# Batch 0's second attention by halves of the columns, with a new order of the opening

## The chip, the cores and the metric

The kernel runs on one core of a Trainium2 chip. The metric is the time of one execution on the device in microseconds (us), the median of several runs.

## The reference

Two stages follow each other. The first is an attention with packed keys: for 8 batches, 8 heads, 576 positions and a head width of 64, a set of 32 packed queries `p` attends to `k` and `v`, and then `q` attends to the packed result, which serves as keys and as values. The second is an MLP over the 4608 tokens of width 512 that the attention gives.

```python
scale = 1.0 / np.sqrt(q.shape[-1])
p_packed = softmax(scale * p @ k.T) @ v             # 8 x 8 x 32 x 64
x = softmax(scale * q @ p_packed.T) @ p_packed      # 8 x 8 x 576 x 64
x = x.transpose(0, 2, 1, 3).reshape(4608, 512)
h = x @ w_in                                        # 512 x 2048
g = s * np.maximum(h, 0.0) ** 2 + b
out = g @ w_out                                     # 2048 x 512
```

## The kernel before

The core works batch by batch. Everything on TensorE is in bf16. The last product of the attention is folded into the MLP: the packed result times `w_in` is formed first (`pw`, 2 x 128 rows, one for each packed query of each head, by 2048 columns), and the MLP's first layer then multiplies `pw` with the softmax weights `aT` (2 x 128 rows by 576 positions). The two halves of the 256 rows are called `qd` 0 and 1 in the code.

The order of the work of batches 0 to 2, and of the attention of batch 3, is written out as a string of words, `ORDER` (line 15). A loop (line 678) calls one function for each word. Each engine executes its own instructions in the order of the words; waits between engines come from the data and from the buffers. The numbers behind a word are the batch and a part. The words that matter here:

| word | function | what it does |
|---|---|---|
| kf, kc | load_first_k, cast_first_k | heads 0 to 3 of batch 0's k, as f32 through SP's queue, and its conversion on DVE and ACT |
| kh, k, q, v, qh | load, load_pairs | loads through POOL's queue, converted to bf16 on the way; qh.0.0 and qh.0.1 are four loads of two heads each |
| p, pp2, mask | load_p, twice_p, mask | load of p, its doubling on DVE, the identity for the transposes on POOL |
| win, wout | load_w_in, load_w_out | a quarter of w_in (two loads), a quarter of w_out |
| kT, qT, pT | prep_k, prep_q, prep_p | TensorE transposes, half of the heads each (pT all), and copies out of PSUM on ACT and DVE |
| s | first_scores | scores of the packed queries (24 matmuls) and their exponential on ACT |
| a | packed | packed result and its sums; after the second, `ppc`, `rd` and `rs` on DVE |
| c | second_scores | scores of q against the packed result (16 matmuls) into two PSUM tiles, one for each qd; an exponential of 576 columns on ACT for each |
| w | weights | for one qd: sums over each head by a matmul with ones, `ld` (logarithm) and `rcd` (exponential of its negative) on ACT, and the product `aT` on DVE |
| e | packed_w1 | a quarter of `pw`: 8 matmuls; qd 0 is scaled out of PSUM by ACT, qd 1 by DVE |
| E | packed_w | half of `pw` |
| m | mlp_in | 128 of the 2048 hidden columns for 576 positions: 4 matmuls of 288 columns, a Relu (`rlu`) on ACT, its square into `gT` on DVE |
| t | Out.step | two of the 16 matmuls (512 columns each) that give 128 rows of the output; after the last, DVE adds the bias and SP's queue stores |
| b | bias_step | two of the 16 matmuls of the bias row |
| four, three | four, three | a change of the PSUM tiles: at "four" one of the two rings of buffers goes over to three output tiles and the bias |
| qo, qD, kD, vo | order_q, dma_q, dma_k, order_v | reordering on DVE and transposes by DMA on SP's queue, for batches from 3 on |
| z | idle | one matmul of zeros, 512 columns, whose result nobody reads (not in the order before) |

PSUM tiles for all but the outputs come from `big()` (line 108), which takes two rings of two buffers in turn; after "four" one ring of two buffers is left, and after "three" there is one of three. A tile's buffer is free when its last reader is done. The raw q, k and v lie in five buffers (line 120), which are given in the order of the words to the next load when the batch's transposes, or the packed result, have used them.

For batch 0 the order before has c.0 (both qd, all columns), then w.0.0 and w.0.1 by qd, with the e's in between. Every m.0 sums over both qd, so it reads what both w's have written.

```python
mm(hps[:, hf, 0:HS], pw[b][:, qd, m * P:(m + 1) * P],
   aT[b][:, qd, hf * HS:(hf + 1) * HS], start=(qd == 0), stop=(qd == NQ - 1))
```

After the last word a loop over batches 3 to 7 (line 682) goes on with a fixed interleaving, which the change leaves alone. It begins with the first m of batch 3 and then s.4.0.

Of the kernel before, what the change touches and what calls it, by code (L numbers as in the profile page):

```python
# [7 lines left out]
F32 = mybir.dt.float32  # L8
BF16 = mybir.dt.bfloat16
AF = mybir.ActivationFunctionType  # L10
ALU = mybir.AluOpType
# [1 line left out]


ORDER = """
kf kh.0.1 p.0.1 kc v.0 mask kT.0.0 qh.0.0 qh.0.1 pp2.0.1 kT.0.1 pT.0 win.0 s.0.0 s.0.1 a.0.0 win.2
qT.0.0 qT.0.1 p.1.2 a.0.1 c.0 w.0.0 e.0.0 win.1 win.3 wout.0 k.1 w.0.1 e.0.1 q.1 wout.1 e.0.2 m.0.3
pp2.1.2 m.0.0 e.0.3 wout.2 m.0.7 m.0.1 m.0.12 m.0.15 m.0.10 m.0.5 m.0.2 v.1 m.0.14 sb four b.0
kT.1.0 t.2 kT.1.1 t.1 m.0.4 qT.1.0 wout.3 b.1 qT.1.1 t.2 b.2 m.0.6 m.0.13 b.3 m.0.11 k.2 q.2 p.2.8
pT.1 t.0 t.1 t.0 b.4 s.1.0 t.1 s.1.1 t.2 m.0.8 b.5 a.1.0 m.0.9 a.1.1 b.6 t.0 c.1 b.7 t.0 t.1 q.3  # L20
kT.2.0 e.1.0 t.2 t.1 w.1.0 pp2.2.8 v.2 t.1 k.3 t.0 w.1.1 qT.2.1 t.0 t.1 t.0 t.0 e.1.1 t.2 kT.2.1 t.2
t.1 t.2 t.2 m.1.0 m.1.3 v.3 three t.3 t.3 pT.2 e.1.2 m.1.2 qT.2.0 t.3 t.3 m.1.1 m.1.5 m.1.7 t.3
e.1.3 m.1.9 qo.3 qD.3 kD.3 s.2.0 t.3 t.4 k.4 m.1.14 pT.3 t.4 m.1.4 s.2.1 t.3 m.1.13 m.1.15 m.1.6
m.1.8 t.4 m.1.11 m.1.10 m.1.12 a.2.0 t.4 t.4 t.3 a.2.1 t.4 t.4 c.2 t.5 t.4 t.5 q.4 E.2.0 t.6 t.5
w.2.0 t.6 w.2.1 s.3.0 t.5 pT.4 t.6 t.6 vo.3 s.3.1 t.5 t.5 m.2.2 m.2.3 t.6 E.2.1 m.2.1 t.6 t.5 v.4
a.3.0 t.5 m.2.5 a.3.1 t.6 m.2.0 t.7 m.2.15 qo.4 t.7 m.2.4 m.2.9 t.7 qD.4 m.2.7 t.7 c.3 t.7 t.6 m.2.6
kD.4 m.2.14 m.2.10 m.2.13 t.7 w.3.0 t.8 t.7 t.8 E.3.0 t.8 t.7 t.8 w.3.1 t.8 E.3.1 t.8 m.2.11 vo.4
t.8 t.8 m.2.12 m.2.8
"""

@with_exitstack
def kernel(
# [21 lines left out]
    B, H, S, D = q.shape  # L54
    NP = p.shape[2]
    DM = H * D
    DFF = moe_w_in.shape[1]
    P = 128
    scale = 1.0 / float(D) ** 0.5

    R = 96
    NC = S // R
    CP = NC // 2
    HP = H // 2
    NQ = H // 4
# [4 lines left out]
    HS = S // 2  # L70
# [6 lines left out]
    attp = ctx.enter_context(tc.tile_pool(name="attp", bufs=1))  # L77
    atp = ctx.enter_context(tc.tile_pool(name="atp", bufs=2))
    smp = ctx.enter_context(tc.tile_pool(name="smp", bufs=2))
    ppw = ctx.enter_context(tc.tile_pool(name="ppw", bufs=2))  # L80
    ysp = ctx.enter_context(tc.tile_pool(name="ysp", bufs=3))
# [10 lines left out]
    def mm(*a, **kw):  # L92
        return tc.keep_in_program_order(nc.tensor.matmul(*a, **kw))  # L93

    def tr(*a, **kw):
        return tc.keep_in_program_order(nc.tensor.transpose(*a, **kw))  # L96
# [9 lines left out]
    vec, act, pool, sp = (Pinned(e) for e in (nc.vector, nc.scalar, nc.gpsimd, nc.sync))  # L106

    def big(dt=F32):
        w = NB if dt == F32 else 2 * NB
        rings["n"] += 1  # L110
        ps = rings["h"][rings["n"] % len(rings["h"])]
        return ps.tile([P, 2, w], dt, tag="h", name="hps")


    kn, qn, vn = {}, {}, {}
# [7 lines left out]
    def raw(name, b):  # L123
        if (name, b - 1) in mine and b > 3:
            mine[name, b] = mine[name, b - 1]
        else:
            mine[name, b] = spare.pop(0)
        return bufs[mine[name, b]][:]

    def give(name, b):  # L130
        if b < 3:
            spare.append(mine[name, b])
# [3 lines left out]
    def done(name, b):  # L136

        halves[name, b] = halves.get((name, b), 0) + 1
        if halves[name, b] == 2:
            give(name, b)  # L140
# [9 lines left out]
    def load_pairs(store, src, b, tag, half):  # L150

        if half == 0:
            store[b] = raw(tag, b).rearrange("r (h x) -> r h x", h=H)
        for h2 in range(2):
            h0 = HP * h2 + 2 * half
            pool.dma_start(
                out=store[b][:, h0:h0 + 2, :],
                in_=src[b, h0:h0 + 2].rearrange("h (r c) d -> r h (c d)", c=NC),
            )

    w_in_sb = wpool.tile([P, NKC, DFF], BF16, name="w_in_sb")
    w_out_sb = wpool.tile([P, NFF, NB], BF16, name="w_out_sb")
    gT = wpool.tile([P, NFF, 3 * S], BF16, name="gT")
# [32 lines left out]
    identb = constp.tile([P, P], BF16, name="identb")  # L196
# [7 lines left out]
    kT = [constp.tile([P, KW], BF16, name=f"kT{i}") for i in range(2)]  # L204
    qT = [constp.tile([P, NC, HP, R], BF16, name=f"qT{i}") for i in range(2)]
    pbd = [constp.tile([P, NQ, 4, 2, NP], BF16, name=f"pbd{i}") for i in range(2)]
    ppc = [constp.tile([P, HP, NP], BF16, name=f"ppc{i}") for i in range(2)]
# [6 lines left out]
    onesbd = constp.tile([P, P], BF16, name="onesbd")  # L214
# [16 lines left out]
    aT, pw, vr, qr, e1, e2, rd, rs = {}, {}, {}, {}, {}, {}, {}, {}  # L231
# [53 lines left out]
    def prep_q(b, half):  # L285
# [18 lines left out]
                vec.tensor_copy(out=dst, in_=src)  # L304
        done("qn", b)

    def dma_q(b):
        sp.dma_start_transpose(
            out=qT[b % 2][:].rearrange("p c h r -> p (c h) r"),
            in_=qr[b][:].rearrange("r c h x d -> r (c h x d)"),  # L310
        )
# [101 lines left out]
    def weights(b, qd):  # L413
# [8 lines left out]
        act.activation(out=rcd[:], in_=ld[:].rearrange("p a s -> p (a s)"), func=AF.Exp, scale=-1.0)  # L422
        vec.tensor_tensor(out=aT[b][:, qd, :], in0=e2[b][:, qd, :], in1=rcd[:], op=ALU.mult)

    def packed_mm(i, ch, outs):

        for hp in range(HP):
            for h2 in range(2):
                mm(
                    outs[h2][NP * hp:NP * hp + NP, :],  # L430
                    ppc[i][D * h2:D * h2 + D, hp, :],
                    w_in_sb[D * h2:D * h2 + D, hp, ch * NB:(ch + 1) * NB],
                    start=True,
                    stop=True,
                    tile_position=(D * h2, NP * hp),
                )
# [15 lines left out]
    def packed_w1(b, ch, on_act=True):  # L452

        i = b % 2
        if ch == 0:
            pw[b] = ppw.tile([P, NQ, DFF], BF16, tag="pw", name="pw")
        t = big()
        packed_mm(i, ch, [t[:, qd, :] for qd in range(NQ)])
        dst = pw[b][:, :, ch * NB:(ch + 1) * NB]
        if on_act:  # L460
            act.activation(out=dst[:, 0], in_=t[:, 0, :], func=AF.Copy, scale=rd[b][:, 0:1])
        else:
            vec.tensor_scalar_mul(out=dst[:, 0], in0=t[:, 0, :], scalar1=rd[b][:, 0:1])
        vec.tensor_scalar_mul(out=dst[:, 1], in0=t[:, 1, :], scalar1=rd[b][:, 1:2])
# [4 lines left out]
    def slot(b):  # L469
        return 1 if b % 2 else (b % 4)  # L470
# [5 lines left out]
    def mlp_in(b, m, on_act=True):  # L476
        hps = big()
        for qd in range(NQ):
            for hf in range(2):
                mm(  # L480
                    hps[:, hf, 0:HS],
                    pw[b][:, qd, m * P:(m + 1) * P],
                    aT[b][:, qd, hf * HS:(hf + 1) * HS],
                    start=(qd == 0),
                    stop=(qd == NQ - 1),
                )
        g0 = slot(b) * S
        dst = gT[:, m, g0:g0 + S].rearrange("p (a s) -> p a s", a=2)
        if on_act:
            rlu = ysp.tile([P, 2, HS], BF16, tag="rlu", name="rlu")  # L490
            act.activation(out=rlu[:], in_=hps[:, :, 0:HS], func=AF.Relu)
            vec.tensor_tensor(out=dst, in0=rlu[:], in1=rlu[:], op=ALU.mult)
        else:
            vec.scalar_tensor_tensor(
                out=dst, in0=hps[:, :, 0:HS], scalar=0.0, in1=hps[:, :, 0:HS],
                op0=ALU.max, op1=ALU.mult,
            )

    def bias_part(bps, m0, m1):
        for m in range(m0, m1):  # L500
            mm(bps, onesb[:], w_out_sb[:, m, :], start=(m == 0), stop=(m == NFF - 1))
        if m1 == NFF:
            vec.tensor_scalar_mul(out=biasrep[:], in0=bps, scalar1=bvec[:])
# [109 lines left out]
    y = outs(0) + outs(1) + outs(2)  # L613
# [22 lines left out]
    def constants():  # L636
        sp.dma_start(out=svec[:], in_=moe_s[0:1].unsqueeze(0).to_broadcast([P, 1]))
        sp.dma_start(out=bvec[:], in_=moe_b[0:1].unsqueeze(0).to_broadcast([P, 1]))

    words = {  # L640
        "k": lambda b: load(kn, k, b, "kn"),
        "q": lambda b: load(qn, q, b, "qn"),
# [14 lines left out]
        "pp2": lambda b0, b1: twice_p(b0, min(b1, B)),  # L657
        "pT": prep_p,
        "kT": prep_k,
        "qT": prep_q,  # L660
        "kD": dma_k,
        "qo": order_q,
        "qD": dma_q,
        "vo": order_v,
        "s": first_scores,
        "a": packed,
        "c": second_scores,
        "w": weights,
        "e": packed_w1,
        "E": packed_w,  # L670
        "m": lambda b, m: mlp_in(b, m),
        "n": lambda b, m: mlp_in(b, m, False),
        "t": lambda t: y[t].step(2),
        "b": bias_step,
# [7 lines left out]
    for b in range(3, B):  # L682
        a = b + 1
        c = a + 1
# [23 lines left out]
        for m in range(NFF):  # L708
            mlp_in(b, m)
            for f in steps.get(m, []):  # L710
                f()
            run_outs(todo, per)
# [33 lines left out]
```

## Time and profile before

| | |
|---|---|
| time, median of 7 runs | 259.12 us (258.93 to 259.52) |
| the profiled execution: its own time | 258.93 us |
| its span in the profile | 257.1 us |
| TensorE (PE) busy | 240.7 us, 94% |
| ScalarE (ACT) busy | 145.3 us, 57% |
| VectorE (DVE) busy | 144.1 us, 56% |
| GpSimd (POOL) busy, mostly issuing loads | 31.4 us, 12% |
| moved by DMA | 34.61 MB, 135 GB/s in the mean |

The span reaches from the first instruction to the last; the execution's own time has 1.8 us more around it. PE is TensorE's matmuls and PEld its loads of weights, which overlap with them. [...]what a group costs is read from the distance between starts. SP's queue and POOL's queue are those that issue transfers. Times in a timeline count from the start of the span.

### The profile page before, as it was taken

The page shows a single profiled execution, that of the slowest core. Times are in us where ns is not written, and L with a number is a line of the kernel's source. Part 1 is how long each engine was busy: PE and PEld are TensorE (multiplying, and loading weights), DVE is VectorE, ACT ScalarE, POOL GpSimd, SP SyncE. Part 2 cuts the span into 40 slices and gives each one's busy share as a digit, 9 for nine tenths or more (in the row PEclk, how much of TensorE's full clock was granted, in tenths as well). Part 3 has the DMA queues.
Part 4 walks back from the last instruction along what each step waited for, and adds up shares of the span by engine and source line. Part 5 has one row for each costly group of instructions (what it writes and reads, how often), then busy time and mean ns, then how long its engine had stood idle before and what let it go on. Part 6 is the DMA issues. An engine that isn't in the chain of part 4 may idle for free.

```text
span 257.1 us, 5606 instructions
## 1 busy us (share of the span) xinstructions
PE 240.7 (94%) x2320; PEld 138.2 (54%) x2320; DVE 144.1 (56%) x299; ACT 145.3 (57%) x220; POOL 31.4 (12%) x47
## 2 busy tenths in 40 slices
PE   1476999999999999999999999999999999999994
PEld 1461556556655664665566455655565555555443
DVE  3324853576765877857854668366835473444212
ACT  3038946456848688848763674569554764444000
POOL 8366230110002100300030003000000000000000
PEclk9999999999999999999999999999999999999999
DMA  5999999999398969993979397946611113111332
GB/s 108 180 204 203 204 206 205 198 199 247 75 160 132 174 133 163 158 234 79 187 101 220 96 177 120 236 91 134 135 43 41 43 41 87 41 41 41 84 82 82
DMA packets 54858, 34.61 MB, mean 135 GB/s; under 512 B 27568, under 2 KB 50352, under 8 KB 54832
## 3 DMA queue, kind: packets, MB, share of 16 engines
q0 software_dynamic: 24864, 18.32, 48.2%
q1 hardware_dynamic: 29872, 15.87, 27.4%
q8 instruction: 18, 0.29, 0.4%
q10 hardware_dynamic: 96, 0.07, 0.1%
q14 instruction: 8, 0.07, 0.1%
HBM read 37.23 MB, written 9.44 MB: 181 GB/s over the span
## 4 chain that ended last, share of the span: by engine, by line
PE 84%; DMA 13%; POOL 1%; issue 1%; DVE 0%; POOLq 0%
PE yps L93 50%; PE hps L93 33%; DMA w_out_sb<-in_moe_w_out_dram 6%; DMA w_in_sb<-in_moe_w_in_dram 4%; DMA raw<-in_k_dram 3%; PE hps L96 1%; POOL raw L104 1%; POOL w_in_sb L104 0%; DVE ysb L104 0%; POOLq L730 0%
## 5 line engine op out<-in xcount | busy, mean ns | idle before, releaser
L93 PE MATMUL yps<-w_out_sb,gT 128*128 128x512 bf16 (+2 forms) x592 | 144.6, 374 | 0.0
L104 ACT ACTIVATE rlu<-hps 128x576 bf16<-128x576 f32 x128 | 80.8, 651 | 63.2 <-PE hps L93 57.2
L104 DVE TENSOR_TENSOR gT<-rlu 128x576 bf16<-128x576 bf16 x128 | 58.2, 457 | 62.0 <-ACT rlu L104 60.0
L93 PE MATMUL hps<-aT,pw 128*128 128x288 bf16 x512 | 81.1, 289 | 0.1
L93 PEld LDWEIGHTS <-gT 128*128 128x128 bf16 x592 | 53.2, 98 | 48.6 <-issue 6.4
L93 PEld LDWEIGHTS <-pw 128*128 128x128 bf16 x512 | 49.8, 99 | 33.9 <-issue 1.3
L104 DVE SCALAR_TENSOR_TENSOR ysb<-yps,svec,biasrep 128x512 f32<-128x512 f32 (+2 forms) x37 | 27.0, 732 | 16.6 <-PE yps L93 16.5
L104 DVE TENSOR_SCALAR pw<-hps,rd 128x1024 bf16<-128x1024 f32 (+1 forms) x20 | 21.3, 1067 | 2.4 <-ACT pw L104 2.0
L104 ACT ACTIVATE pw<-hps,rd 128x1024 bf16<-128x1024 f32 (+1 forms) x20 | 18.7, 942 | 4.5 <-PE hps L93 3.7
L104 DVE TENSOR_TENSOR aT<-e,rcd 128x576 bf16<-128x576 bf16 x16 | 12.1, 758 | 13.1 <-ACT rcd L104 13.1
L104 POOL DMA_DIRECT2D raw<-in_k_dram x8 | 6.4, 802 | 94.4 <-DMA kT<-raw 83.5
L96 PE MATMUL hps<-identb,raw 96*64 96x96 bf16 (+1 forms) x216 | 9.9, 232 | 8.1 <-DVE raw L104 5.8
L104 ACT ACTIVATE e<-hps 96x768 bf16<-96x768 f32 x16 | 12.6, 800 | 8.1 <-PE hps L93 8.1
L104 ACT ACTIVATE e<-hps,rs 128x576 bf16<-128x576 f32 x16 | 11.0, 738 | 6.4 <-PE hps L93 6.4
L96 PEld LDWEIGHTS <-raw 96*64 96x64 bf16 (+1 forms) x216 | 8.5, 123 | 10.7 <-DVE raw L104 5.8
L93 PE MATMUL hps<-w_in_sb,ppc 64*32 64x512 bf16 x256 | 12.1, 410 | 1.4 <-DMA w_in_sb<-in_moe_w_in_dram 1.4
L104 ACT ACTIVATE rcd<-ld 128x576 f32<-128x576 f32 x16 | 10.9, 682 | 0.5
L104 ACT ACTIVATE ld<-hps 128x576 f32<-128x576 f32 x16 | 10.3, 646 | 1.2 <-PE hps L93 1.0
L104 DVE COPY raw<-raw 96x1536 bf16<-96x1536 bf16 x20 | 10.4, 562 | 0.0
L93 PEld LDWEIGHTS <-raw 96*64 96x64 bf16 (+1 forms) x264 | 8.4, 113 | 2.9 <-issue 2.1
L93 PE MATMUL hps<-e,raw 96*64 96x32 bf16 (+1 forms) x264 | 9.2, 194 | 0.8 <-ACT e L104 0.8
L93 PE MATMUL hps<-pbd,kT 128*128 128x64 bf16 x192 | 8.6, 199 | 1.1 <-DVE pbd L104 1.1
(41 smaller groups left out, 97.8 us busy)
## 6 DMA issues: line engine op xcount, KB each, us to landing
raw<-in_v_dram POOLq DMA_DIRECT2D x8, 576.0 KB, 12.2
out_dram<-ysb SPq DMA_DIRECT2D x23, 192.0 KB, 2.3
raw<-in_k_dram POOLq DMA_DIRECT2D x7, 576.0 KB, 6.7
raw<-in_q_dram POOLq DMA_DIRECT2D x7, 576.0 KB, 10.4
out_dram<-ysb SPq DMA_DIRECT2D x24, 128.0 KB, 2.4
w_in_sb<-in_moe_w_in_dram POOLq DMA_DIRECT2D x8, 256.0 KB, 9.4
w_out_sb<-in_moe_w_out_dram POOLq DMA_DIRECT2D x4, 512.0 KB, 16.5
out_dram<-ysb SPq DMA_DIRECT2D x23, 64.0 KB, 2.2
```

The source lines that it names most:

```text
L93: return tc.keep_in_program_order(nc.tensor.matmul(*a, **kw))
L96: return tc.keep_in_program_order(nc.tensor.transpose(*a, **kw))
L104: return lambda *a, **kw: tc.keep_in_program_order(f(*a, **kw))
```

## The change

Three things change.

For batch 0 the second scores and the softmax weights are made by halves of the columns instead of by qd. `second_scores_half` makes one half's scores for both qd in one PSUM tile (8 matmuls) and two exponentials of 288 columns. `weights_half` makes the sums, the logarithm, the reciprocal and the product of one half's columns for both qd. The word c.0 becomes c.0.0 and c.0.1, and w.0.0 and w.0.1 now stand for the halves. The words h.0.0 to h.0.15 replace m.0.0 to m.0.15: `mlp_in_half` takes 256 hidden columns for one half of the positions (h.0.x with even x for the first half), 4 matmuls of 288 columns, one Relu and one square each, as an m has.

For batch 0, qT goes by halves of the columns, all heads at once (`prep_q_chunks`); the loads of q stay four loads of two heads.

The order of the words is another up to the end of the string. In the opening the loads of q stand ahead of v, the quarters of w_in come in the order 0, 1, 2, 3, p.1.2 stands behind k.1, kT.0.1 is ahead of kT.0.0, and six idle matmuls (z) are added. f.0.0 and f.1.2 do the work of e.0.0 and e.1.2 with both qd scaled on DVE. Later, the loads of batches 2 and 3 come as q.2, k.2, p.2.8, q.3, v.3, k.3, v.2.

```diff
--- before.py
+++ after.py
@@ -13,19 +13,19 @@
 
 
 ORDER = """
-kf kh.0.1 p.0.1 kc v.0 mask kT.0.0 qh.0.0 qh.0.1 pp2.0.1 kT.0.1 pT.0 win.0 s.0.0 s.0.1 a.0.0 win.2
-qT.0.0 qT.0.1 p.1.2 a.0.1 c.0 w.0.0 e.0.0 win.1 win.3 wout.0 k.1 w.0.1 e.0.1 q.1 wout.1 e.0.2 m.0.3
-pp2.1.2 m.0.0 e.0.3 wout.2 m.0.7 m.0.1 m.0.12 m.0.15 m.0.10 m.0.5 m.0.2 v.1 m.0.14 sb four b.0
-kT.1.0 t.2 kT.1.1 t.1 m.0.4 qT.1.0 wout.3 b.1 qT.1.1 t.2 b.2 m.0.6 m.0.13 b.3 m.0.11 k.2 q.2 p.2.8
-pT.1 t.0 t.1 t.0 b.4 s.1.0 t.1 s.1.1 t.2 m.0.8 b.5 a.1.0 m.0.9 a.1.1 b.6 t.0 c.1 b.7 t.0 t.1 q.3
-kT.2.0 e.1.0 t.2 t.1 w.1.0 pp2.2.8 v.2 t.1 k.3 t.0 w.1.1 qT.2.1 t.0 t.1 t.0 t.0 e.1.1 t.2 kT.2.1 t.2
-t.1 t.2 t.2 m.1.0 m.1.3 v.3 three t.3 t.3 pT.2 e.1.2 m.1.2 qT.2.0 t.3 t.3 m.1.1 m.1.5 m.1.7 t.3
-e.1.3 m.1.9 qo.3 qD.3 kD.3 s.2.0 t.3 t.4 k.4 m.1.14 pT.3 t.4 m.1.4 s.2.1 t.3 m.1.13 m.1.15 m.1.6
-m.1.8 t.4 m.1.11 m.1.10 m.1.12 a.2.0 t.4 t.4 t.3 a.2.1 t.4 t.4 c.2 t.5 t.4 t.5 q.4 E.2.0 t.6 t.5
-w.2.0 t.6 w.2.1 s.3.0 t.5 pT.4 t.6 t.6 vo.3 s.3.1 t.5 t.5 m.2.2 m.2.3 t.6 E.2.1 m.2.1 t.6 t.5 v.4
-a.3.0 t.5 m.2.5 a.3.1 t.6 m.2.0 t.7 m.2.15 qo.4 t.7 m.2.4 m.2.9 t.7 qD.4 m.2.7 t.7 c.3 t.7 t.6 m.2.6
-kD.4 m.2.14 m.2.10 m.2.13 t.7 w.3.0 t.8 t.7 t.8 E.3.0 t.8 t.7 t.8 w.3.1 t.8 E.3.1 t.8 m.2.11 vo.4
-t.8 t.8 m.2.12 m.2.8
+z kf kc kh.0.1 mask p.0.1 qh.0.0 qh.0.1 kT.0.1 kT.0.0 z z v.0 z win.0 win.1 pp2.0.1 pT.0 qT.0.1 z
+s.0.0 s.0.1 qT.0.0 win.2 a.0.0 a.0.1 c.0.0 f.0.0 sb win.3 c.0.1 w.0.0 w.0.1 e.0.1 z h.0.2 h.0.0
+e.0.2 wout.0 q.1 h.0.4 h.0.7 h.0.5 e.0.3 h.0.6 h.0.8 wout.1 h.0.1 h.0.11 h.0.13 k.1 h.0.3 four
+h.0.10 t.1 p.1.2 h.0.9 wout.2 t.2 h.0.15 qT.1.1 t.1 t.2 qT.1.0 b.0 t.0 h.0.12 t.0 v.1 b.1 pp2.1.2
+t.1 kT.1.1 t.2 pT.1 wout.3 b.2 h.0.14 q.2 kT.1.0 t.1 t.0 t.0 b.3 s.1.0 s.1.1 t.0 t.1 k.2 t.1 p.2.8
+a.1.0 b.4 a.1.1 q.3 b.5 b.6 b.7 c.1 t.1 t.0 t.1 e.1.0 w.1.0 t.0 t.0 w.1.1 v.3 t.2 qT.2.1 t.2 e.1.1
+k.3 t.2 t.2 t.2 kT.2.0 pp2.2.8 m.1.0 three t.3 t.3 pT.2 kT.2.1 f.1.2 t.3 e.1.3 v.2 t.3 qT.2.0 t.3
+m.1.8 m.1.1 m.1.6 m.1.14 m.1.13 m.1.3 t.3 m.1.5 m.1.10 qo.3 m.1.2 t.4 qD.3 s.2.0 m.1.7 m.1.9 m.1.11
+t.4 s.2.1 m.1.4 m.1.12 kD.3 t.3 m.1.15 a.2.0 t.4 a.2.1 t.4 t.4 t.4 pT.3 k.4 c.2 t.4 t.4 t.3 E.2.0
+w.2.0 t.6 t.6 t.5 w.2.1 t.6 t.5 t.5 vo.3 t.6 E.2.1 t.6 m.2.5 t.5 t.5 t.6 pT.4 t.6 s.3.0 s.3.1 t.6
+m.2.1 t.5 m.2.3 a.3.0 m.2.13 t.5 m.2.10 a.3.1 t.7 q.4 t.7 t.7 c.3 t.5 qo.4 m.2.2 t.7 t.7 w.3.0 t.8
+t.8 E.3.0 qD.4 t.8 t.8 kD.4 w.3.1 v.4 t.7 m.2.14 t.7 m.2.0 m.2.15 m.2.6 m.2.7 m.2.9 t.8 t.8 m.2.12
+m.2.8 m.2.11 t.7 m.2.4 E.3.1 t.8 t.8 vo.4
 """
 
 @with_exitstack
@@ -157,6 +157,16 @@
                 out=store[b][:, h0:h0 + 2, :],
                 in_=src[b, h0:h0 + 2].rearrange("h (r c) d -> r h (c d)", c=NC),
             )
+
...
     w_in_sb = wpool.tile([P, NKC, DFF], BF16, name="w_in_sb")
     w_out_sb = wpool.tile([P, NFF, NB], BF16, name="w_out_sb")
@@ -298,6 +308,28 @@
         for x in range(2):
             dst = qT[i][:, :, 2 * half + x, :]
             src = tp[:, x, 0:S].rearrange("p (c r) -> p c r", c=NC)
+            if x == 0:
+                act.copy(out=dst, in_=src)
+            else:
+                vec.tensor_copy(out=dst, in_=src)
+        done("qn", b)
+
+    def prep_q_chunks(b, hf):
+
+        i = b % 2
+        tp = big(BF16)
+        for hp in range(HP):
+            for c in range(CP):
+                o = ((hp % 2) * CP + c) * R
+                for h2 in range(2):
+                    tr(
+                        tp[D * h2:D * h2 + D, hp // 2, o:o + R],
+                        qn[b][:, hp + HP * h2, (CP * hf + c) * D:(CP * hf + c + 1) * D],
+                        identb[0:R, 0:R],
+                    )
+        for x in range(2):
+            dst = qT[i][:, CP * hf:CP * hf + CP, 2 * x:2 * x + 2, :].rearrange("p c a r -> p a c r")
+            src = tp[:, x, 0:S].rearrange("p (a c r) -> p a c r", a=2, c=CP)
             if x == 0:
                 act.copy(out=dst, in_=src)
             else:
@@ -422,6 +454,46 @@
         act.activation(out=rcd[:], in_=ld[:].rearrange("p a s -> p (a s)"), func=AF.Exp, scale=-1.0)
         vec.tensor_tensor(out=aT[b][:, qd, :], in0=e2[b][:, qd, :], in1=rcd[:], op=ALU.mult)
 
+    def second_scores_half(b, hf):
+
+        i = b % 2
+        if hf == 0:
+            e2[b] = attp.tile([P, NQ, S], BF16, tag="e2", name="e2")
+        t = big()
+        for hp in range(HP):
+            for h2 in range(2):
+                mm(
+                    t[NP * hp:NP * hp + NP, h2, 0:HS],
+                    ppc[i][D * h2:D * h2 + D, hp, :],
+                    qT[i][D * h2:D * h2 + D, CP * hf:CP * hf + CP, hp, :],
+                    start=True,
+                    stop=True,
+                    tile_position=(D * h2, NP * hp),
+                )
+        for qd in range(NQ):
+            act.activation(
+                out=e2[b][:, qd, hf * HS:(hf + 1) * HS],
+                in_=t[:, qd, 0:HS],
+                func=AF.Exp,
+                scale=rs[b][:, qd:qd + 1],
+            )
+
+    def weights_half(b, hf):
+        if hf == 0:
+            aT[b] = atp.tile([P, NQ, S], BF16, tag="aT", name="aT")
+        cols = slice(hf * HS, (hf + 1) * HS)
+        dps = big()
+        for qd in range(NQ):
+            mm(dps[:, qd, 0:HS], onesbd[:], e2[b][:, qd, cols], start=True, stop=True)
+        ld = smp.tile([P, 2, HS], F32, tag="ld", name="ld")
+        act.activation(out=ld[:], in_=dps[:, :, 0:HS], func=AF.Ln)
+        rcd = smp.tile([P, S], F32, tag="rcd", name="rcd")
+        act.activation(out=rcd[:], in_=ld[:].rearrange("p a s -> p (a s)"), func=AF.Exp, scale=-1.0)
+        vec.tensor_tensor(
+            out=aT[b][:, :, cols], in0=e2[b][:, :, cols],
+            in1=rcd[:].rearrange("p (a s) -> p a s", a=2), op=ALU.mult,
+        )
+
     def packed_mm(i, ch, outs):
 
         for hp in range(HP):
@@ -495,6 +567,25 @@
                 out=dst, in0=hps[:, :, 0:HS], scalar=0.0, in1=hps[:, :, 0:HS],
                 op0=ALU.max, op1=ALU.mult,
             )
+
+    def mlp_in_half(b, x):
+
+        mp, hf = divmod(x, 2)
+        hps = big()
+        for y in range(2):
+            m = 2 * mp + y
+            for qd in range(NQ):
+                mm(
+                    hps[:, y, 0:HS],
+                    pw[b][:, qd, m * P:(m + 1) * P],
+                    aT[b][:, qd, hf * HS:(hf + 1) * HS],
+                    start=(qd == 0),
+                    stop=(qd == NQ - 1),
+                )
+        g0 = slot(b) * S + hf * HS
+        rlu = ysp.tile([P, 2, HS], BF16, tag="rlu", name="rlu")
+        act.activation(out=rlu[:], in_=hps[:, :, 0:HS], func=AF.Relu)
+        vec.tensor_tensor(out=gT[:, 2 * mp:2 * mp + 2, g0:g0 + HS], in0=rlu[:], in1=rlu[:], op=ALU.mult)
 
     def bias_part(bps, m0, m1):
         for m in range(m0, m1):
@@ -637,6 +728,7 @@
         sp.dma_start(out=svec[:], in_=moe_s[0:1].unsqueeze(0).to_broadcast([P, 1]))
         sp.dma_start(out=bvec[:], in_=moe_b[0:1].unsqueeze(0).to_broadcast([P, 1]))
 
+    by_halves = (0,)
     words = {
         "k": lambda b: load(kn, k, b, "kn"),
         "q": lambda b: load(qn, q, b, "qn"),
@@ -644,6 +736,7 @@
         "kh": lambda b, x: load(kn, k, b, "kn", 4 * x, 4 * x + 4),
         "qh": lambda b, x: load_pairs(qn, q, b, "qn", x),
         "vh": lambda b, x: load_pairs(vn, v, b, "vn", x),
         "kf": load_first_k,
         "kc": cast_first_k,
         "p": lambda b0, b1: load_p(b0, min(b1, B)),
@@ -657,18 +750,20 @@
         "pp2": lambda b0, b1: twice_p(b0, min(b1, B)),
         "pT": prep_p,
         "kT": prep_k,
-        "qT": prep_q,
+        "qT": lambda b, x: (prep_q, prep_q_chunks)[b in by_halves](b, x),
         "kD": dma_k,
         "qo": order_q,
         "qD": dma_q,
         "vo": order_v,
         "s": first_scores,
         "a": packed,
-        "c": second_scores,
-        "w": weights,
+        "c": lambda b, *x: (second_scores, second_scores_half)[b in by_halves](b, *x),
+        "w": lambda b, x: (weights, weights_half)[b in by_halves](b, x),
         "e": packed_w1,
+        "f": lambda b, ch: packed_w1(b, ch, False),
         "E": packed_w,
         "m": lambda b, m: mlp_in(b, m),
+        "h": mlp_in_half,
         "n": lambda b, m: mlp_in(b, m, False),
         "t": lambda t: y[t].step(2),
         "b": bias_step,
```

## The prediction

> **What bounds the kernel now.** I read the busy table and the slices first, then the chain of waits, then the timeline of the first 50 us, engine by engine. The page says that TensorE (PE) is the bound, and where it is not:
>
> ```profile
> PE 240.7 (94%) x2320; PEld 138.2 (54%) x2320; DVE 144.1 (56%) x299; ACT 145.3 (57%) x220; POOL 31.4 (12%) x47
> PE   1476999999999999999999999999999999999994
> ```
>
> Each slice is 6.4 us: after the fourth, PE is full to the end. The chain (start, us, what) says the same: transfers until 37.6 us, then PE.
>
> ```profile
> 1.30 7.76 DMA raw<-in_k_dram
> ...
> 9.95 10.03 DMA w_in_sb<-in_moe_w_in_dram
> ...
> 21.98 15.59 DMA w_out_sb<-in_moe_w_out_dram
> 37.61 0.59 PE yps L93 x2
> ```
>
> So the time is the PE work plus what PE loses in the opening. The timeline (start, us, engine, ...) shows the loss:
>
> ```profile
> 18.49 0.68 PE L93 MATMUL hps<-qT,ppc 64*32 64x288 bf16 x16 [0.56 <-DVE ppc L104]
> 19.23 1.37 ACT L104 ACTIVATE e<-hps,rs 128x576 bf16<-128x576 f32 x2 [1.49 <-PE hps L93]
> 22.10 0.76 DVE L104 TENSOR_TENSOR aT<-e,rcd 128x576 bf16<-128x576 bf16 x1 [3.38 <-ACT rcd L104]
> 23.93 0.76 DVE L104 TENSOR_TENSOR aT<-e,rcd 128x576 bf16<-128x576 bf16 x1 [0.41 <-ACT rcd L104]
> 24.76 2.10 PE L93 MATMUL hps<-aT,pw 128*128 128x288 bf16 x8
> 27.35 4.54 PE L93 MATMUL hps<-aT,pw 128*128 128x288 bf16 x32
> 28.23 4.61 ACT L104 ACTIVATE rlu<-hps 128x576 bf16<-128x576 f32 x8
> ```
>
> c.0 starts at 18.49, and no m.0 can start until both weight tiles (aT) are there, at 24.69. From 24.76 PE is busy, but the first matmuls of 288 columns come 240 ns apart (8 take 2.0 us) and only from 27.7 on 122 ns: half clock. Further small losses are waits for q.1 (0.3 us at 34.7) and w_out (0.4 at 37.2). By c.1, at 47.28, PE has done about 25.8 us of work in warm slots, so 21.5 us are lost by then; hardly anything after. A warm slot, from the timeline's start-to-start distances, is m 0.49 us, t and b 0.43, kT 0.51, qT 0.6, s 0.35, a 0.65, e 0.35, w 0.25.
>
> [...]240 against 122 ns, the switch 2.9 us after the m's begin. [...]from 13.98 to 17.93 us PE was never idle, half of it transposes, and stayed at half clock. [...]the POOL loads do land in their order of issue.[...]
>
> **The loads.** POOL has eight loads out at once (win.0's second half is issued at 9.34, after the first load landed at 9.06), and from 10 to 45 us the ring is never empty: the stage table has 201 to 205 GB/s there. So a load's landing is the sum of what is ahead of it. The trace's landings: kh 9.06, p 9.26, v 12.09, the four q parts 12.83 to 15.03, win 17.65, 20.93, 23.73, 26.35, wout.0 28.87, k.1 32.27, q.1 34.96, wout.1 37.56, wout.2 40.09, v.1 42.96, wout.3 45.49. Reordered: q parts by 12.2, v 15.0, win.0 17.65, win.1 20.9, win.2 23.5, win.3 26.1 (p.1.2, 0.24, goes back), wout.0 28.6, q.1 31.9, wout.1 34.5, k.1 37.3, wout.2 40.1, v.1 43.0, wout.3 45.5. The mask moved ahead of p delays issues by 0.3 us, nothing else, as kh is still in flight.
>
> **The change part by part, in cold slots until the clock switches.**
> 1. Before c.0.0. kT.0.1 now comes first and waits for kh: PE starts at 9.1, two kT (0.96 each) to 11.03, three idle matmuls (0.43 each) to 12.3, pT to 12.5, qT.0.1 to 13.5, idle to 13.9, two s (0.64 each) to 15.2, qT.0.0 to 16.2. The exponentials (2 x 0.8) end at 16.3, a.0.0 and a.0.1 (0.95 each) at 18.25, ppc and rs as before 0.7 to 0.9 later: c.0.0 at 18.9. **0.4 later than now**; of the six added idle matmuls (2.6 us) only the one before s, 0.43, is on the path, the others stand in gaps.
> 2. The halves. c.0.0 has 8 matmuls for 16; its two exponentials of 288 elements[...] run 19.4 to 20.3, those of c.0.1 20.2 to 21.05[...]. w.0.0 at 20.3, logarithm 21.05, reciprocal 21.7 to 22.4, product (0.76) to **23.2**: half of the columns for both qd. w.0.1 is done at 24.5. f.0.0 puts 0.7 us from ACT onto idle DVE. So h.0.2 starts at 23.25 against 24.76: **1.5 us earlier**.
> 3. h.0.2 and h.0.0 take 1.92 cold. e.0.2 then waits for a buffer: that of e.0.1, which DVE empties only after the second product, at 25.2. e.0.2 to 25.8, h.0.4 to 26.8. I let the clock switch at 27.0 (3.7 us after the h's start). Then h.0.7, h.0.5, e.0.3, h.0.6, h.0.8, h.0.1 run to 29.75. An h needs one 576-element Relu as an m does (0.575 apart on ACT against 0.49 on PE), so ACT paces; h.0.11 waits 0.45 for e.0.3's copies, and after "four", with two buffers left, t.1 starts at 32.2, qT.1.1 at 34.05, b.0 at 36.1.
> 4. From there slots add up, no load being late (kT.1.1 at 38.7 against k.1 37.3, a.1.0 at 45.0 against 43.0, b.6 at 47.2 against 45.5): c.1 at **48.05**. By then 14 t's and 8 b's are done, now 9 and 7: 6 x 0.43 = 2.6 us more work. The same work is done now at 47.28 + 2.6 = 49.9. **Gain 1.85 us.** Matmul work stays as it was (16 h are 128 matmuls, as 16 m).
> 5. Behind c.1 the order is new, and PE stays full if nothing is late. v.2 moves behind v.3 and k.3 and takes kT.2.1's buffer: issued at 57.6, landing some 10 us later as v.3 does now (56.5 to 66.4), needed by a.2.0 at 70.9. On SP, qD.4 and kD.4 stand behind t.5's stores: about 92.5, landed 101 (3.1 + 5.1), needed by s.4.0 at 103.6 (82.6 us of slots ahead of it and 21 lost); now 102.5 for 105.3. I cost these at nothing, on margins of 3 and 2.5 us; f.1.2 too, with DVE at 7.6 of 10 us there. The tail is untouched.
>
> The switch is the term that no row settles. At 30.7 nothing is left of the gain (each us of half clock costs 0.5). In the other direction, if the idle matmuls bring it by 18 us, a, c, w and the first h's run warm: some 1.3 us more. I take 27.0.
>
> Sum: the profiled execution, 258.93 (span 257.1 and 1.8 around it), becomes 257.1; the median of the runs is 0.2 above it: 257.3.
>
> **The rivals.**
> - Main case, 57%: 257.3 (256.5 to 258.4).
> - Early clock, 16%: the idle matmuls and s keep PE busy from 9.1 to 16.2. For it: no gap there, where now there are three. Against: over half of it are transposes (kT and qT, 3.9 of 7.1 us), and a similar stretch did not do it. 256.0.
> - The halves do not come apart, 12%: h.0.2 waits for the whole of aT, to 24.5, so 1.2 of the 1.5 us go and 258.4 is left, up to no change. Against: now w.0.0's matmuls start at 20.02 with the second exponential running to 20.6, and m.0.3 starts while e.0.2's part of pw is unwritten: waits go by region.
> - Slower, 15%: the clock stays low through the h's. PE pauses before e.0.2, h.0.11 and at the ACT-paced buffers[...]. The loss starts to outweigh the gain at a switch after 30.7; at 34 it is 3.5 - 1.85, so 260.8. For it: the h's are paced by ACT, more than the m's. Against: the pause before h.0.11 is 0.45 us[...].
>
> **How the numbers follow.** A measurement of this kernel can tell about 0.2% (0.5 us) from no change. Faster: the main case, the early clock and a small part of the third, 0.75; same 0.11; slower 0.14. From 255.6 (early clock, with its cost unknown by 0.4) to 259.5 (third case, late switch) lie some 8 in 10.
>
> **What would show it.** c.0.0 near 18.9; the first matmuls of aT and pw near 23.3 and before the second product ends; spacing 122 ns from about 27; c.1 near 48; no PE wait for a load after 38 us. First aT matmuls at 24.5 or later, a switch beyond 30, or a wait on v.2 or kT.4 would make it wrong.

## The result and the profile after

The kernel after takes **257.43 us** in the median (256.04 to 258.54) against 259.08 (258.62 to 259.53) for the kernel before beside it: a ratio of 0.9935, 95% interval 0.9921 to 0.9949, so 1.7 us less (0.0065 of 259.08; the other gains below are worked out in the same way). The forecast was 257.3. The profiled execution took 256.43, with a span of 254.7, and is one of the shorter ones: it is 2.5 us below the profiled execution of the kernel before.

The busy table and the slices of the kernel after:

```profile
PE 240.1 (94%) x2326; PEld 137.4 (54%) x2326; DVE 145.4 (57%) x301; ACT 143.4 (56%) x220; POOL 31.4 (12%) x47
PE   0588999999999999999999999999999999999994
PEclk9997999999999999999999999999999999999999
```

PE has what it had, plus the six idle matmuls, and its second to fourth slices went from 4, 7, 6 to 5, 8, 8. The fourth slice of the clock is new: a 7.

Lines of the timeline (start, us, engine, ...) of the kernel after, chosen from the stretch that the prediction shows for the kernel before:

```profile
18.27 0.32 PE L93 MATMUL hps<-qT,ppc 64*32 64x288 bf16 x8 [0.38 <-DVE ppc L104]
18.66 1.68 ACT L104 ACTIVATE e<-hps,rs 128x288 bf16<-128x288 f32 x4 [1.78 <-PE hps L93]
21.62 0.76 DVE L104 TENSOR_TENSOR aT<-e,rcd 128x576 bf16<-128x576 bf16 x1 [1.34 <-ACT rcd L104]
22.43 2.07 PE L93 MATMUL hps<-aT,pw 128*128 128x288 bf16 x8
22.88 0.76 DVE L104 TENSOR_TENSOR aT<-e,rcd 128x576 bf16<-128x576 bf16 x1 [0.50 <-ACT rcd L104]
24.78 1.64 PE L93 MATMUL hps<-aT,pw 128*128 128x288 bf16 x12
26.61 0.41 PE L93 MATMUL hps<-w_in_sb,ppc 64*32 64x512 bf16 x8 [0.19 <-DVE pw L104]
28.81 2.12 PE L93 MATMUL hps<-aT,pw 128*128 128x288 bf16 x16 [0.22 <-DVE pw L104]
47.17 0.44 PE L93 MATMUL hps<-qT,ppc 64*32 64x288 bf16 x16
```

The first product ends at 22.38, and PE starts on it at 22.43, while the second product runs from 22.88 to 23.64. Before, PE started on aT at 24.76, after both products. Ahead of e.0.3 (at 26.61) stand 20 matmuls of aT and pw, before there were 8. c.1 starts at 47.17 with 14 t's and 8 b's done. In the kernel before it started at 47.28, with 9 and 7 done:

```profile
47.28 0.52 PE L93 MATMUL hps<-qT,ppc 64*32 64x288 bf16 x16
```

That is 2.6 us more work by then, so the opening gained 2.7. From c.1 to the end of the span 207.5 us remain, here and in four of the profiles of the new order below. The 209.8 of before less that work would be 207.2, so the later order gave back 0.3.

The chain of waits of the kernel after (start, us, what) leads to the first h's through one engine after the other:

```profile
16.40 1.50 PE hps L93 x59
...
17.92 0.30 DVE ppc L104
...
18.27 0.36 PE hps L93 x8
...
18.66 1.68 ACT e L104 x4
20.33 0.55 ACT ld L104
...
20.91 0.69 ACT rcd L104
...
21.62 0.77 DVE aT L104
```

Each link is half as wide as the whole batch: the scores of c.0.0 for half of the columns, their exponentials and those of c.0.1 one behind the other, then logarithm, reciprocal and product of the first half.

After 38 us the list of waits of the kernel after (what waits, on what: us in total, times, longest) has one entry in which a matmul waits, and it is no load:

```profile
PE yps L93 <- DVE ysb L104: 0.2, 1, 0.2
```

### The profile page after: what moved, and what is told of

It reads as the page before. It is cut to its first block, busy times and chain, and to the rows that moved or that the text cites. A ratio compares the mean times of both kernels' runs of the same rounds, so it can differ in the third digit from the quotient of the medians.

```text
span 254.7 us, 5625 instructions
## 1 busy us (share of the span) xinstructions
PE 240.1 (94%) x2326; PEld 137.4 (54%) x2326; DVE 145.4 (57%) x301; ACT 143.4 (56%) x220; POOL 31.4 (12%) x47
## 4 chain that ended last, share of the span: by engine, by line
PE 91%; DMA 3%; ACT 3%; DVE 1%; issue 1%; POOLq 0%
PE yps L93 51%; PE hps L93 36%; PE hps L96 3%; DMA raw<-in_k_dram 3%; ACT e L104 1%; ACT rlu L104 1%; DVE ysb L104 0%; ACT pw L104 0%; DVE aT L104 0%; DVE pw L104 0%; ACT rcd L104 0%; ACT ld L104 0%; DVE ppc L104 0%; POOLq L104 0%; POOLq L825 0%
## 5 line engine op out<-in xcount | busy, mean ns | idle before, releaser
L104 DVE TENSOR_SCALAR pw<-hps,rd 128x1024 bf16<-128x1024 f32 (+1 forms) x22 | 22.5, 1036 | 1.0 <-PE hps L93 0.4
L104 ACT ACTIVATE pw<-hps,rd 128x1024 bf16<-128x1024 f32 (+1 forms) x18 | 17.5, 973 | 3.8 <-PE hps L93 3.7
L104 ACT ACTIVATE e<-hps,rs 128x576 bf16<-128x576 f32 (+1 forms) x18 | 11.3, 686 | 10.1 <-PE hps L93 10.1
L96 PEld LDWEIGHTS <-raw 96*64 96x64 bf16 (+1 forms) x216 | 8.2, 117 | 10.6 <-DMA raw<-in_k_dram 8.1
L93 PE MATMUL hps<-w_in_sb,ppc 64*32 64x512 bf16 x256 | 11.4, 388 | 0.3 <-DVE pw L104 0.2
L104 ACT COPY qT<-hps 128x576 bf16<-128x576 bf16 x6 | 3.8, 635 | 9.6 <-PE hps L96 9.6
L93 PEld LDWEIGHTS <-raw 96*64 96x64 bf16 (+1 forms) x264 | 7.7, 106 | 2.5 <-issue 2.0
L93 PE MATMUL hps<-e,raw 96*64 96x32 bf16 (+1 forms) x264 | 8.6, 188 | 0.4 <-ACT e L104 0.4
## 6 DMA issues: line engine op xcount, KB each, us to landing
w_in_sb<-in_moe_w_in_dram POOLq DMA_DIRECT2D x8, 256.0 KB, 10.1
```

What stands on the lines that cost most here:

```text
L104: return lambda *a, **kw: tc.keep_in_program_order(f(*a, **kw))
```

## The experiments

The change has three parts: the halves, the order with its loads, and the idle matmuls. My theory was that the halves bring the gain, because the first h's start earlier. The rivals were that the order brings it, or that the idle matmuls do, through the clock. The first four runs take one part away, or do one part alone.

**The kernel after without its six idle matmuls**

```diff
-z kf kc … kT.0.0 z z v.0 z win.0 … qT.0.1 z s.0.0 … e.0.1 z h.0.2
+kf kc … kT.0.0 v.0 win.0 … qT.0.1 s.0.0 … e.0.1 h.0.2
```

> The kernel after without its six idle matmuls, all else as it is. Theory H (the halves bring the h's forward by some 1.5 us; the idle matmuls only add to it in those executions in which they switch the clock early): TensorE's clock switches once, 3 to 4 us after the first h as in the kernel before, c.0.0 starts near 18.5, and the time is 257.0 to 257.8, with a spread between executions below 1 us instead of 2.5. Rival Z (the idle matmuls and the early clock make most of the gain): the time goes back to 258.6 or more.

Measured: 257.80 us (256.82 to 258.14), ratio 0.9949 [0.9934, 0.9963]. Its timeline:

```profile
22.71 2.10 PE L93 MATMUL hps<-aT,pw 128*128 128x288 bf16 x8 [1.09 <-DVE aT L104]
...
25.31 2.59 PE L93 MATMUL hps<-aT,pw 128*128 128x288 bf16 x12
```

In the profiled execution the clock goes up once, at 27.27, and c.1 starts at 48.41. That is the opening which the prediction worked out for the kernel after (27.0 and 48.05). Three quarters of the gain is left: the idle matmuls are not its main source, but they do not cost anything either. The spread, 1.3 us, is above the 1 us that was expected.

**The kernel after, batch 0 by qd as before**

```diff
-by_halves = (0,)
+by_halves = ()
-c.0.0 f.0.0 sb win.3 c.0.1 … h.0.2 h.0.0 …
+c.0 f.0.0 sb win.3 … m.0.2 m.0.0 …
```

> The kernel after with batch 0 by qd again (c.0, w.0.0 and w.0.1 by qd, m.0.x in the places of h.0.x, qT by heads); order, loads and idle matmuls stay. Theory H: the first m waits for both products and starts 1.2 to 1.5 us later than the first h, so 258.3 to 259.0. Rival Z: nothing much changes, 257.0 to 257.9, because the clock switches as early as now. Rival O (order and loads alone): also 257.0 to 257.9, and then the run without idle matmuls stays there too.

Measured: 258.22 us (256.62 to 259.37), ratio 0.9965 [0.9949, 0.9981], between the two expectations. Its timeline:

```profile
22.71 0.41 PE L93 MATMUL hps<-aT,pw 128*128 128x288 bf16 x2 [0.73 <-DVE aT L104]
23.96 0.90 PE L93 MATMUL hps<-aT,pw 128*128 128x288 bf16 x6 [0.85 <-DVE aT L104]
```

The first m starts on qd 0 and stops after two matmuls, for the second product. This is the step that the halves take away. But without them 0.9 us of the 1.7 is still there, so the order and the idle matmuls together count for as much as they do.

**The halves alone, in the order before**

```diff
-c.0 w.0.0 … m.0.3 pp2.1.2 m.0.0 e.0.3 …
+c.0.0 c.0.1 w.0.0 … h.0.2 pp2.1.2 h.0.0 e.0.3 …
```

> The kernel before with the halves alone: c.0.0 and c.0.1 in the place of c.0, w by halves, h's in the places of the m's of batch 0 (h.0.2 first), qT by halves of the columns; order of all other words, loads and no idle matmuls as before. Theory H: the first h starts 1.0 to 1.5 us before the 24.76 of the first m unless e.0.1 and e.0.2, which stand ahead of it and wait for w_in until 23.7, hold it; so 0.5 to 1.2 us are gained: 257.9 to 258.6. Rivals Z and O: 259.1 within 0.3.

Measured: 259.11 us (258.57 to 259.49), ratio 1.0003 [0.9994, 1.0011]: nothing. Its timeline says why the halves' lead is not used:

```profile
22.95 0.61 PE L93 MATMUL hps<-w_in_sb,ppc 64*32 64x512 bf16 x1 [0.90 <-DMA w_in_sb<-in_moe_w_in_dram]
24.19 1.05 PE L93 MATMUL hps<-w_in_sb,ppc 64*32 64x512 bf16 x15 [0.64 <-DMA w_in_sb<-in_moe_w_in_dram]
25.17 2.10 PE L93 MATMUL hps<-aT,pw 128*128 128x288 bf16 x8
```

e.0.1 stands ahead of the first h and waits for win.1, which comes after win.2 in this order. The h's start at 25.17, although the first product ended at 23.27 (22.51 and 0.76). c.0.0 is late too, at 19.03 against 18.49: qT by halves of the columns needs all four loads of q, and the last landed at 15.92. In the new order q stands ahead of v, and its last load landed at 12.37.

**The idle matmuls alone, in the order before**

```diff
-kf kh.0.1 … kT.0.1 pT.0 … s.0.0 … m.0.3
+z kf kh.0.1 … kT.0.1 z z z pT.0 … z s.0.0 … z m.0.3
```

> The kernel before with six idle matmuls alone (one at the start, three behind kT.0.1, one ahead of s.0.0, one ahead of the first m). Theory H: [...]the clock is at half rate again when the m's start, in most executions; 258.7 to 259.5. Rival Z: clock switched before 20 us and 257.3 to 258.0.

Measured: 259.19 us (258.60 to 259.86), ratio 1.0009 [1.0001, 1.0017]. In the profiled execution the clock went up at 13.19, but was back at half from 16.60 to 26.84. The first m started at 25.25. The idle matmuls alone bring no gain.

So the halves and the idle matmuls are each worth nothing alone in the order before, and the halves are worth 0.8 in the new one (0.9965 less 0.9935). The next four runs asked what in the new order lets them count, and how much a clock that is up through the first h's would bring.

**The kernel after with more idle matmuls**

```diff
-z kf kc …  a.0.1 c.0.0 …  w.0.0 …  e.0.1 z h.0.2
+Z.22 kf kc …  a.0.1 Z.2 c.0.0 …  z w.0.0 …  e.0.1 Z.3 h.0.2      # Z.n: n idle matmuls
```

> The kernel after with the clock held up: 22 idle matmuls in place of the first (they end before the first transposes at 9.4 us), two more behind a.0.1, one ahead of w.0.0, three in place of the one ahead of h.0.2. Theory C (the 2.5 us between executions of the kernel after are the clock's windows, up early and falling back for one to three windows between 17 and 28 us): clock at full rate before 10 us and not down again, all executions within 0.6 us of each other, and as the first h's run at 122 instead of 240 ns the time is 255.5 to 256.2, below the best of the kernel after by a little. Rival: the spread has another cause (loads, or the start of the queues); then it stays above 1.5 us and the median near 257.4.

Measured: **256.23 us** (256.03 to 256.64), ratio 0.9895 [0.9882, 0.9907]. The median is below that of both kernels. Its four executions lie within 0.6 us, where those of the kernel after differ by 2.5. Its timeline:

```profile
22.62 1.14 PE L93 MATMUL hps<-aT,pw 128*128 128x288 bf16 x8 [0.67 <-DVE aT L104]
24.53 1.64 PE L93 MATMUL hps<-aT,pw 128*128 128x288 bf16 x12
```

The first eight h matmuls take 1.14 us, not 2.07. The clock was up from 6.22 on, except from 16.46 to 19.87. The expectation had it up throughout.

**The same idle matmuls, by qd** (the edit above on the kernel by qd)

> The same idle matmuls in the new order with batch 0 by qd (no halves). With the clock out of play the difference to the run before this one is what the halves are worth. Theory H: the first m ends its wait 1.2 us later than the first h, but at full clock two h's are only 1.0 us of work and e.0.2 waits for e.0.1's copies at 25 us in both, so 0.3 to 0.7 us more: 256.1 to 256.8. Rival: halves worth their whole 1.3 us also here, 257 or more.

Measured: 257.00 us (256.26 to 258.22), ratio 0.9928 [0.9909, 0.9947], above the 256.1 to 256.8 of theory H; c.1 at 47.61 against 46.77 by halves. Its six executions still differ by 2.0 us. With these, the runs make a table of the new order (ratio to the kernel before, median us):

| new order | by qd | by halves |
|---|---|---|
| no idle matmuls | 0.9980 [0.9970, 0.9991], 258.45 | 0.9949 [0.9934, 0.9963], 257.80 |
| the six | 0.9965 [0.9949, 0.9981], 258.22 | 0.9935 [0.9921, 0.9949], 257.43 |
| more of them | 0.9928 [0.9909, 0.9947], 257.00 | 0.9895 [0.9882, 0.9907], 256.23 |

In each row the halves are worth 0.8 to 0.9 us (0.0030 to 0.0033 of 259). The six idle matmuls bring 0.4 in each column, where the intervals still overlap, so that this part is not told apart from nothing. More of them bring another 1.0. The upper left cell is the last of the runs:

```diff
-z kf kc … c.0.0 … h.0.2 h.0.0 …
+kf kc … c.0 … m.0.2 m.0.0 …
```

> The kernel after by qd and without idle matmuls: its order and loads alone. With the three others of this square (halves and idle matmuls 257.4, halves alone 257.8, idle matmuls alone 258.2): if the parts add, 258.5 to 258.9; if the order makes no gain without one of the others, 259.0 or more.

Measured: 258.45 us (257.05 to 259.78). The order and the loads alone bring 0.5. Which of their moves do it was not taken apart.

**The order before with win.1 ahead of win.2**, by halves and by qd; e.0.2 goes behind the first two of the h's, or of the m's:

```diff
-a.0.0 win.2 … win.1 win.3 … e.0.1 q.1 wout.1 e.0.2 m.0.3 pp2.1.2 m.0.0 e.0.3
+a.0.0 win.1 … win.2 win.3 … e.0.1 q.1 wout.1 h.0.2 pp2.1.2 h.0.0 e.0.2 e.0.3   # or m.0.3, m.0.0
```

> The kernel before with the halves, win.1 loaded ahead of win.2, and e.0.2 behind the first two h's; no idle matmuls. It tests why the halves alone brought nothing: e.0.1 waited for win.1 until 24.2 and stood ahead of the first h. If that is the cause, e.0.1 is done by 22.0, the first h starts near 23.3 instead of 25.2, and the time is 257.8 to 258.5. If the halves are worth nothing in the old order for another reason (q's loads behind v, the order of t and b behind), 258.8 to 259.3.

> The kernel before with only that: win.1 ahead of win.2 and e.0.2 behind m.0.3 and m.0.0; no halves, no idle matmuls. Theory H: the m's still wait for the second product at 24.7, so 258.7 to 259.2. Rival O (loads and order make the gain, the halves none): as the run before this one, 258.5 or less.

Measured: 259.06 us (258.73 to 259.44), ratio 0.9999 [0.9991, 1.0007], by halves; 259.39 (258.78 to 260.42), ratio 1.0013 [1.0004, 1.0021], by qd. The two differ by 0.4 us, but their intervals overlap. The timeline by halves:

```profile
23.12 0.40 PE L93 MATMUL hps<-aT,pw 128*128 128x288 bf16 x1 [0.82 <-DVE aT L104]
23.69 1.86 PE L93 MATMUL hps<-aT,pw 128*128 128x288 bf16 x7 [0.17 <-DVE pw L104]
25.48 1.37 PE L93 MATMUL hps<-w_in_sb,ppc 64*32 64x512 bf16 x16
26.79 5.45 PE L93 MATMUL hps<-aT,pw 128*128 128x288 bf16 x32
```

The first h now starts 1.6 us earlier than m.0.3 did before, and still nothing is gained. The h's behind e.0.3 start at 26.79, 0.6 earlier than before, but run at half clock until 29.59 (before until 27.75), 1.8 us longer, and half of those 1.8 us is lost (240 against 122 ns from start to start). So the start of the first h by itself is no measure of the gain. I then took the landing of wout.1 (theory D in the expectations) to be what holds this order back: everything up to b.0 can only come together when the t's can run.

**The same with idle matmuls, with earlier loads of w_out in the order before, and with both**

```diff
+Z.12 kf …  kT.0.0 Z.6 …  kT.0.1 z z …  z s.0.0 …  a.0.1 Z.2 …  z w.0.0 …  e.0.1 Z.3   # idle
-… k.1 w.0.1 e.0.1 q.1 wout.1 …
+… kh.1.0 w.0.1 e.0.1 wout.1 kh.1.1 q.1 …   # loads; kT.1.1 behind m.0.13, qT.1.x behind s.1.x
```

> The run with the halves in the old order and win.1 ahead of win.2, now with idle matmuls that hold the clock up (12 at the start, 6 behind kT.0.0, two behind kT.0.1, one ahead of s.0.0, two behind a.0.1, one ahead of w.0.0, three behind e.0.1). Theory D (in the old order the landing of wout.1 at 37.5 us, behind k.1 and q.1, is the bound; TensorE is no more than 0.7 us behind it, so what it gains before is lost in the wait of b.2): first h near 23 us at full rate, TensorE waits 2 us or more for q.1 and wout.1 instead of 0.7, b.2 still at 37.5, time 258.5 to 259.2. Rival S (the sum of what TensorE loses sets the end, as the prediction worked it): 2 to 3 us of gain, 256.3 to 257.3.

> The kernel before with other loads alone: q.1 and the second half of k.1 behind wout.1, so that wout.1 lands near 33.0 instead of 37.6, with kT.1.1 moved behind m.0.13 and qT.1.0 and qT.1.1 behind t.1 and t.2 of s.1.0 and s.1.1. No halves, no idle matmuls. Theory D: the waits of 0.7 us go and no more, since TensorE is late by itself: 258.2 to 258.8. Rival S: the same 0.7. If the loads alone are the gain: 257.5 or less.

> The two runs before this one together: halves, win.1 first, clock held up, and wout.1 ahead of q.1 and of half of k.1. Theory D: with both bounds moved the gain appears, 1.7 to 2.8 us: 256.3 to 257.4, with v.1 (landing near 42.6) as the next bound. If halves and loads merely add (0 and 0.5), 258.5.

Measured: 259.08 us (258.75 to 259.57), ratio 1.0005 [0.9997, 1.0013]; 259.75 (259.66 to 260.05), 1.0030 [1.0019, 1.0041]; 259.89 (259.59 to 260.87), 1.0038 [1.0025, 1.0051]. Theory D fell. The first of these times lies where it put it, but the waits of 2 us that it forecast are not there: the kernel with idle matmuls has no wait for wout.1 and gains nothing. With wout.1 earlier (landed at 33.23) the time gets longer, which no theory had forecast. In its timeline what was moved back is late next: wout.2 is waited for, 0.48 us at 40.16. With both changes that wait is gone and the time is no shorter, so why these loads cost time stays open. The timeline of the kernel with idle matmuls shows what stays:

```profile
23.69 1.14 PE L93 MATMUL hps<-aT,pw 128*128 128x288 bf16 x8 [1.21 <-DVE pw L104]
25.18 0.59 PE L93 MATMUL hps<-w_in_sb,ppc 64*32 64x512 bf16 x9 [0.35 <-ACT rlu L104]
27.10 0.41 PE L93 MATMUL hps<-w_in_sb,ppc 64*32 64x512 bf16 x7 [1.33 <-DMA w_in_sb<-in_moe_w_in_dram]
27.44 5.76 PE L93 MATMUL hps<-aT,pw 128*128 128x288 bf16 x32
```

Clock and halves put the first eight h matmuls at 23.69 to 24.8. Then e.0.3 waits 1.33 us for win.3, all other h's stand behind it, and from 27.55 to 30.97 the clock is down again. In the order before, only two m's or h's stand ahead of e.0.3, and the others start behind it (starts in us, one execution each):

| order before | first m or h | those behind e.0.3 | clock full from |
|---|---|---|---|
| before | 24.76 | 27.35 | 27.75 |
| halves | 25.17 | 27.77 | 30.17 |
| idle matmuls | 25.25 | 27.50 | 26.84 |
| win.1 first, by halves | 23.12 | 26.79 | 29.59 |
| win.1 first, by qd | 23.31 | 27.56 | 30.35 |
| win.1 first, halves, idle | 23.69 | 27.44 | 30.97 |

From the latest to the earliest, the starts in the second column differ by 2.1 us and those in the third by 1.0. Some 0.5 us of that difference is e.0.2, which stands behind the first two in the last three rows (e.0.0 of the kernel before took 0.56 at half rate). The rest is pauses: by qd 1.10 us for the second product, in the last row 1.33 for win.3.

How late the clock comes can be read from the stretches of 3.41 us that end with its rise: its changes lie that far apart, or a multiple of it (6.82 and 3.42 us in the kernel after, 3.41 and 10.24 with the idle matmuls alone). In these six profiles PE was busy in them for 2.98 to 3.41 us; in the stretch before, which pauses had broken, for 1.74 to 2.88 us. By halves with win.1 first, 2.88 of the 3.42 us from 22.76 to 26.18 did not raise it, and 3.41 of the next 3.41 did. From these I estimate that a pause among the first h's can put the rise off by a whole stretch. Counted in steps of 3.41 from the start of the span, the six rises lie some 0.3 to 3.1 us behind a step: where the stretches begin differs from profile to profile, so the last column is partly chance.

In the new order h.0.4, h.0.7 and h.0.5 stand between e.0.2 and e.0.3, and fill PE from 24.78 until win.3 has landed (25.99). That this place of e.0.3 is what the halves need is the reading that fits these starts. A kernel with e.0.3 alone moved back in the order before was not run, so this is argued and not shown.

## Why the prediction was right

The sum came out: 257.3 forecast, 257.43 measured, inside the range. Its terms came out less evenly, and that it is within 0.13 is in part luck. The kernel without idle matmuls, whose clock goes up once in its profile, as in the main case, takes 257.80, 0.5 above the forecast. The 0.4 us between it and the kernel after go with an earlier clock, which the main case does not have.

1. **c.0.0.** It started at 18.27, forecast 18.9. The 0.43 us of idle matmul "on the path" was the term with the wrong sign. With the clock at full rate from 14.13 to 20.95 in this execution, a and w ran at full rate (23 matmuls of a.0.0 in 0.53 us, before in 0.77). Without the idle matmuls c.0.0 stands at 18.42, 9.30 us after the first transposes instead of 8.84, and the median is 0.4 longer.
2. **The halves.** The products end at 22.38 and 23.64, 0.8 to 0.9 earlier than forecast, with about the 1.3 us between them that was forecast. The waits do go by region, as PE starts on aT at 22.43 and the second product ends at 23.64: the third rival is out. But "1.5 us earlier" was put down to the halves, and that is the step that was wrong in its cause. The start of the first h is not what they are worth. They bring 0.8 to 0.9 in the new order, in three pairs of kernels, in the order before 0.0 alone, and 0.4 with overlapping intervals where win.1 comes first. One exponential of a half takes 502 ns, one of 576 columns 738 in the kernel before; the four overlap and took 1.68 us, 0.42 each, where the forecast had 0.45 a piece, which was my estimate.
3. **The h's.** e.0.2 came at 24.43, forecast 25.2, and h.0.11 waits 0.22 for e.0.3's copies, forecast 0.45. The term that no row settled, the clock at 27.0, fits the kernel without idle matmuls (27.27). The kernel after was full from 24.37 in the profiled execution, after half rate from 20.95. b.0 at 34.94 and c.1 at 47.17 are earlier by 1.2 and 0.9 for that.
4. **The loads.** They landed within 0.7 us of the forecast (win.1 21.09 for 20.9, wout.1 33.98 for 34.5, wout.3 45.09 for 45.5), and none is waited for after 38 us.
5. **Behind c.1.** v.2 was issued at 57.34 and landed at 65.96; no wait on it, nor on qD.4 or kD.4. The later order, costed at nothing, cost 0.3 us in this profile; the one wait that the list shows there is 0.2 us, of a t for ysb.

The main case has the clock go up once, at 27.0. No execution of the kernel after did that, and the mean granted clock shows it. In the profiles half rate is on record only after a first rise (at 14.13 in the kernel after, at 27.75 in the one before): in the opening, or at the very end of the span (from 256.44 in the kernel before). There it takes little off the mean: no execution of the kernel before is below 0.997. In the profiled execution the mean is 0.993, and the records show half rate from 20.95 to 24.37; 3.42 us at half rate in a span of 254.7 are 0.7%, which gives this 0.993. By the same working 0.987 stands for two such stretches and 0.980 for three.

| mean clock of the kernel after | executions | us |
|---|---|---|
| 0.993 | 6 | 256.04 to 256.56 |
| 0.984 to 0.987 | 5 | 257.13 to 258.16 |
| 0.980 | 4 | 258.45 to 258.54 |

So by this reading the clock had risen early and fallen again in all fifteen. The first row comes near the 256.0 of the "early clock" rival, though the first h's ran at half rate in the profiled execution, which that rival had at full rate. The median lies near the main case's value because the executions spread over all three rows. The fourth rival, a clock that stays low through the h's, comes nearest to the last row, where 0.6 us of the gain is left; no execution of this kernel came near its 260.8. Only one of the fifteen was profiled, so where the stretches lay in the others is not shown, and the mean alone does not always order the times: by qd with six idle matmuls, two executions at 0.993 took 257.91 and 258.08, and three at 0.986 took 257.25 to 257.95.

The order and the loads were priced only through the starts that they allow. Alone they bring 0.5, and with them the halves bring 0.8, which they did not in any form of the order before that was run.

## What to carry to other kernels

A product that comes earlier is worth only as much as the work that stands behind it in program order and can run on it. Before the price of an earlier start is put into a sum, look at what the next blocking word waits for. Here it was a load in two of the kernels that gained nothing (win.1, 0.90 and 0.64 us, with the halves alone; win.3, 1.33 us, with idle matmuls added); that other work ahead of that word is the remedy is argued above and not shown by itself. And where the clock is a term, forecast it as several cases with their own times: the kernel after differs by 2.5 us from execution to execution. More idle matmuls took another 1.0 us off the time. By halves the four executions then lay within 0.6 us; by qd the six still differed by 2.0.

## What the runs showed of the hardware

**The clock falls within the opening.** These are the stretches of the kernel after, cut at the clock's own changes (stretch: length, PE's busy us and number of matmuls, granted clock, share of DMA, GB/s):

```profile
10.72:14.13 3.41, 3.41 (x41) 1.00 1.30 203
14.13:17.54 3.41, 2.87 (x103) 1.00 1.24 205
17.54:20.95 3.41, 2.41 (x43) 1.00 1.24 206
20.95:24.37 3.42, 3.14 (x17) 0.50 1.24 205
```

The clock went up at 14.13, fell at 20.95 and rose at 24.37. (Ahead of the first record, at 14.13, the 1.00 is no reading: the matmuls there run at half rate, 24 transposes of k in 2.10 us from 9.43 on, where at full rate 12 of them took 0.68 at 37.59.) The distances are 6.82 and 3.42 us. The clock fell after a stretch in which PE was busy for 2.41 of 3.41 us. The kernel by qd with the six idle matmuls, whose clock rose at 14.81, kept it over a stretch of the same length with less:

```profile
21.64:25.05 3.41, 1.83 (x22) 1.00 1.24 205
```

So the busy time of a stretch does not say whether the clock falls. What does stays open.

**What warms.** The stretch from 10.72 to 14.13 of the kernel after, with three idle matmuls of 512 columns (1.3 us) between transposes, ended with the clock's rise. Zeros count: with 22 idle matmuls at the start the clock rose at 6.22, before PE had done anything else, and the first 24 transposes, at 9.25, took 1.19 us. In the kernel before PE was busy without a break from 13.98 to 17.93, half of it transposes and the rest small matmuls, and the clock stayed at half. But such an opening can raise it too: of the two kernels in the new order without idle matmuls, 9 of 28 executions have a mean clock of 0.980 to 0.986, and in the profiles with a mean of 0.980 that comes from an early rise and a fall (with the idle matmuls alone a rise at 13.19 and half rate from 16.60 to 26.84). With the six idle matmuls all fifteen executions of the kernel after read 0.993 or less. So the idle matmuls made an early rise more frequent here. How much of them it takes was not looked for.

**Matmuls overlap.** The 512 matmuls of aT and pw last 289 ns each in the mean in the kernel before and 288 in the kernel after, while at full rate their starts come 122 ns apart (16 from 28.81 on take 2.12 us).
